# Tokens on 64 lanes of 7: q on even and k on odd partitions, chunks of 128 keys, one chunk shared by two heads

## The chip, the cores and the metric

One core of one Trainium2 chip. The metric is the device time of one execution in microseconds (us). The engines are called PE (TensorE), DVE (VectorE), ACT (ScalarE), POOL (GpSimd) and SP (SyncE).

## The reference

```python
# q, k, v: (8 batches, 12 heads, 448 tokens, 64); g_q, g_k: (64,)
def rmsnorm(x, g):
    return x / np.sqrt(np.mean(x * x, axis=-1, keepdims=True) + 1e-06) * g
scores = rmsnorm(q, g_q) @ rmsnorm(k, g_k).transpose(0, 1, 3, 2) / 8
attn   = softmax(scores)                       # over the keys
x      = (attn @ v) -> (3584 tokens, 768)
h = x @ w_in                                   # (768, 2048)
out = (h * sigmoid(1.702 * h)) @ w_out         # (2048, 768), float32
```

## The kernel before

The work is cut into 48 units, each two heads of one batch. A unit's q, k and v are loaded as float32, q and k are normed to bf16 and turned (by PE in the first 12 units, by a transposing DMA in the later 36), scores are taken key by query, ACT takes the exponential, PE multiplies with v and a column of ones, DVE divides, and the result is turned back as the input of the two products of the MLP. A list scheduler written into the kernel fixes the order of all instructions on every engine from estimated durations and searched tables of keys. The framework then adds the waits that the data need.

The 448 tokens of a head lie on 112 partitions, four in each. Landing buffers of the first units lie in one large tile, `late`, with turned q and k and with values ready for PE. Later the same tile holds terms of the second product.

```python
late = consts.tile([128, 3 * T_LEN + N_SUM * S_LEN], BF16, name="late", tag="late")
def piece(n, dtype=BF16): ...                   # the next n columns of late
early_raw  = [piece(4 * NS * D, FP32)... for _ in range(2)]   # q/k land here
early_vraw = [piece(2 * NS * D, FP32)... for _ in range(3)]   # v lands here
qkw_ring  += [piece(KW) for _ in range(N_KZ - K_KZ)]          # turned q and k
vx_ring   += [piece(2 * NS * (D + 1))... for _ in range(N_V - K_V)]
# ... cut ...
def load(i, which):
    src = (q, k, v)[which][b, h0:h0 + 2].rearrange("h (ss ns) d -> ss h ns d", ns=NS)
    if which == 2:
        nc.sync.dma_start(out=vraw[...][:SS], in_=src)          # SS = 112
        return
    eng = nc.scalar if i == 0 and which == 1 else nc.sync
    eng.dma_start(out=raw[...][:SS, which], in_=src)
# ... cut ...
def take_q(i):                                  # units turned by PE
    nc.vector.tensor_copy(out=qk_ring[...][:, 0], in_=tps[i][:, 0])
def take_k(i):
    nc.vector.tensor_scalar(out=qk_ring[...][:, 1], in0=tps[i][:, 1],
                            scalar1=gG[:, :], scalar2=None, op0=ALU.mult)
# ... cut ...
def score(u, t):                                # two heads on half the rows each
    for hp in range(2):
        r = slice(64 * hp, 64 * hp + 64)
        nc.tensor.matmul(sc[:, hp, ...], lhsT=qkw[r, k0:k0 + WIN], rhs=qk[r, 0, qs], ...)
```

Of the kernel before, what the change touches and what calls it, by code (L numbers as in the profile page):

```python
# [9 lines left out]
FP32 = mybir.dt.float32  # L10
# [16 lines left out]
class _Order:  # L27
# [36 lines left out]
    def run(self):  # L64
# [32 lines left out]
        def share():  # L97
            n = len(heads())
            return 1.3 / 2 if n == 2 and not queues["sw"] else 1.0 / n

        def next_moved():
            h = heads()
            when = [q[0].there for q in queues.values() if q and q[0].there > moved_to]
            when += [moved_to + t.rest / share() for t in h]
            return min(when) if when else None

        def move_to(now):
            nonlocal moved_to, seq
            while moved_to < now:
# [3 lines left out]
                for t in h:  # L113
                    t.rest -= (until - moved_to) * share()
# [109 lines left out]
    'g': 14.22, 'gT': -28.28, 'gG': 10.29, ('S', 0, 0): 33.65, ('R', 0, 0): -27.2, ('S', 0, 1):  # L224
    11.09, ('R', 0, 1): 12.24, ('Q', 0): 30.36, ('N', 0, 0): -6.12, ('N', 0, 1): -30.37, ('V',
    0): -7.89, ('T', 0, 0): -31.78, ('T', 0, 1): -29.53, ('KQ', 0): -10.97, ('K', 0): -11.43,
    ('S', 1, 0): 9.57, ('R', 1, 0): -27.21, ('S', 1, 1): 33.28, ('R', 1, 1): 9.51, ('Q', 1):
    33.27, ('N', 1, 0): 9.56, ('N', 1, 1): 11.7, ('V', 1): -5.89, ('T', 1, 0): 57.36, ('T', 1,
    1): 54.48, ('KQ', 1): -6.09, ('K', 1): -5.86, ('S', 2, 0): 32.41, ('R', 2, 0): -5.94, ('Q',
    2): 15.94, ('N', 2, 0): -4.94, ('N', 2, 1): -13.33, ('V', 2): 10.47, ('T', 2, 0): 55.3,  # L230
    ('T', 2, 1): 17.1, ('KQ', 2): -6.5, ('K', 2): -4.7, ('S', 3, 0): -3.51, ('R', 3, 0): -11.44,
    ('Q', 3): 33.8, ('N', 3, 0): -27.91, ('N', 3, 1): -14.89, ('V', 3): -5.47, ('T', 3, 0):
    19.15, ('T', 3, 1): 18.23, ('KQ', 3): 58.1, ('K', 3): -9.14, ('S', 4, 0): 33.8, ('R', 4, 0):
    57.84, ('Q', 4): 34.16, ('N', 4, 0): 23.2, ('N', 4, 1): 9.27, ('V', 4): -10.25, ('T', 4, 0):
    -3.92, ('T', 4, 1): 18.9, ('KQ', 4): -7.69, ('K', 4): 59.82, ('S', 5, 0): 18.65, ('R', 5,
    0): -7.68, ('Q', 5): 22.81, ('N', 5, 0): 1.27, ('N', 5, 1): 43.71, ('V', 5): -16.35, ('T',
    5, 0): -40, ('T', 5, 1): 16.66, ('KQ', 5): -8.39, ('K', 5): -9.71, ('L', 6, 0): 54.32, ('L',
    6, 1): 54.14, ('L', 6, 2): 54.15, ('S', 6, 0): -24.61, ('R', 6, 0): -9.13, ('N', 6, 0):
    -16.87, ('N', 6, 1): -1.42, ('V', 6): -24.19, ('T', 6, 0): -37.32, ('T', 6, 1): 56.1, ('KQ',
    6): -17.12, ('K', 6): -15.91, ('L', 7, 0): 55.06, ('L', 7, 1): 57.25, ('L', 7, 2): 55.05,  # L240
    ('S', 7, 0): -17.15, ('R', 7, 0): 31.45, ('N', 7, 0): 3.06, ('N', 7, 1): -23.94, ('V', 7):
    -24.2, ('T', 7, 0): 52.6, ('T', 7, 1): 22.24, ('KQ', 7): -20.86, ('K', 7): 9.99, ('L', 8,
    0): 54.79, ('L', 8, 1): 57.74, ('L', 8, 2): 53.4, ('S', 8, 0): 44.16, ('R', 8, 0): 31.27,
    ('Q0', 8): -1.5, ('Q', 8): -10, ('N', 8, 0): 3.5, ('N', 8, 1): 19.46, ('V', 8): -20.98,
    ('T', 8, 0): 27.35, ('T', 8, 1): 59.99, ('KQ', 8): -20.38, ('K', 8): -21.01, ('L', 9, 0):
    53.95, ('L', 9, 1): 55.46, ('L', 9, 2): 55.45, ('S', 9, 0): -9.31, ('R', 9, 0): -17.4, ('N',
    9, 0): -3.91, ('N', 9, 1): -10.14, ('V', 9): 22.05, ('T', 9, 0): -32.5, ('T', 9, 1): -35.1,
    ('KQ', 9): 21.57, ('K', 9): -38.08, ('L', 10, 0): 57.72, ('L', 10, 1): 59.75, ('L', 10, 2):
    60, ('S', 10, 0): -10.41, ('R', 10, 0): 19.25, ('N', 10, 0): 27.28, ('N', 10, 1): -1.35,
    ('V', 10): -15.43, ('T', 10, 0): -30.6, ('T', 10, 1): -36.19, ('KQ', 10): -4.09, ('K', 10):  # L250
    -37.28, ('L', 11, 0): 59.99, ('L', 11, 1): 59.99, ('L', 11, 2): 55.44, ('S', 11, 0): -13.26,
    ('R', 11, 0): 29.44, ('Q0', 11): 25.43, ('Q', 11): -9.79, ('N', 11, 0): 24.78, ('N', 11, 1):
    3.73, ('V', 11): 3.33, ('T', 11, 0): -37.35, ('T', 11, 1): -37.08, ('KQ', 11): -32.1, ('K',
    11): 24.13, ('C', 0, 0, 0): -31.61, ('E', 0, 0, 0): 59.86, ('C', 0, 0, 1): -26.54, ('E', 0,
    0, 1): 56.76, ('P', 0, 0, 0, 0): 53.97, ('P', 0, 0, 0, 1): -27.58, ('P', 0, 0, 0, 2):
    -30.53, ('P', 0, 0, 0, 3): -27.58, ('O', 0, 0, 0): -5.47, ('B', 0, 0): -40, ('X', 0, 0):
    -11.15, ('C', 1, 0, 0): -26.72, ('E', 1, 0, 0): -2.87, ('C', 1, 0, 1): 57.55, ('E', 1, 0,
    1): 16.48, ('P', 1, 0, 0, 0): 18.9, ('P', 1, 0, 0, 1): 18.63, ('P', 1, 0, 0, 2): 18.63,
    ('P', 1, 0, 0, 3): 18.89, ('O', 1, 0, 0): -13.5, ('B', 1, 0): 20.2, ('X', 1, 0): -11.33,
    ('C', 2, 0, 0): -40, ('E', 2, 0, 0): 18.66, ('C', 2, 0, 1): 20.21, ('E', 2, 0, 1): 13.02,  # L260
    ('P', 2, 0, 0, 0): 15.34, ('P', 2, 0, 0, 1): -36.54, ('P', 2, 0, 0, 2): -39.14, ('P', 2, 0,
    0, 3): -39.14, ('O', 2, 0, 0): -0.47, ('B', 2, 0): -39.81, ('X', 2, 0): -5.02, ('C', 3, 0,
    0): 17.29, ('E', 3, 0, 0): 39.33, ('C', 3, 0, 1): -39.63, ('E', 3, 0, 1): 38.35, ('P', 3, 0,
    0, 0): 15.85, ('P', 3, 0, 0, 1): 43.01, ('P', 3, 0, 0, 2): 17.41, ('P', 3, 0, 0, 3): 18.15,
    ('O', 3, 0, 0): -10.7, ('B', 3, 0): 15.63, ('X', 3, 0): 0.44, ('C', 4, 0, 0): -4.69, ('E',
    4, 0, 0): 38.96, ('C', 4, 0, 1): 38.48, ('E', 4, 0, 1): 24.48, ('P', 4, 0, 0, 0): -33.37,
    ('P', 4, 0, 0, 1): 60, ('P', 4, 0, 0, 2): -31.73, ('P', 4, 0, 0, 3): 17.26, ('O', 4, 0, 0):
    0.31, ('B', 4, 0): 57.93, ('X', 4, 0): 41.32, ('C', 5, 0, 0): -31.71, ('E', 5, 0, 0): 17.88,
    ('C', 5, 0, 1): 15.57, ('E', 5, 0, 1): 35.94, ('P', 5, 0, 0, 0): 33.77, ('P', 5, 0, 0, 1):
    33.77, ('P', 5, 0, 0, 2): 33.77, ('P', 5, 0, 0, 3): 33.76, ('O', 5, 0, 0): -0.04, ('B', 5,  # L270
    0): -23.85, ('X', 5, 0): 33.63, ('C', 0, 1, 0): 14.17, ('E', 0, 1, 0): 39.32, ('C', 0, 1,
    1): -39.73, ('E', 0, 1, 1): 33.79, ('P', 0, 1, 0, 0): -36.96, ('P', 0, 1, 0, 1): -33.38,
    ('P', 0, 1, 0, 2): 60, ('P', 0, 1, 0, 3): -14.87, ('O', 0, 1, 0): 60, ('B', 0, 1): 54.78,
    ('X', 0, 1): 34.24, ('C', 1, 1, 0): -36.97, ('E', 1, 1, 0): -39.74, ('C', 1, 1, 1): -36.95,
    ('E', 1, 1, 1): 24.11, ('P', 1, 1, 0, 0): 33.76, ('P', 1, 1, 0, 1): -23.7, ('P', 1, 1, 0,
    2): -22.7, ('P', 1, 1, 0, 3): -23.86, ('O', 1, 1, 0): -21.46, ('B', 1, 1): -39.64, ('X', 1,
    1): 0.33, ('C', 2, 1, 0): -27.46, ('E', 2, 1, 0): -31.49, ('C', 2, 1, 1): -18.62, ('E', 2,
    1, 1): 37.85, ('P', 2, 1, 0, 0): -39.65, ('P', 2, 1, 0, 1): -40, ('P', 2, 1, 0, 2): 21.69,
    ('P', 2, 1, 0, 3): -40, ('O', 2, 1, 0): -14.64, ('B', 2, 1): -36.82, ('X', 2, 1): -4.18,
    ('C', 3, 1, 0): 55.19, ('E', 3, 1, 0): 37.86, ('C', 3, 1, 1): 60, ('E', 3, 1, 1): 23.18,  # L280
    ('P', 3, 1, 0, 0): -18.63, ('P', 3, 1, 0, 1): -13.68, ('P', 3, 1, 0, 2): -13.69, ('P', 3, 1,
    0, 3): -11.57, ('O', 3, 1, 0): 39.32, ('B', 3, 1): 22.25, ('X', 3, 1): -18.47, ('C', 4, 1,
    0): -15.41, ('E', 4, 1, 0): 9.01, ('C', 4, 1, 1): -25.6, ('E', 4, 1, 1): -9.3, ('P', 4, 1,
    0, 0): -36.38, ('P', 4, 1, 0, 1): -36.83, ('P', 4, 1, 0, 2): -36.39, ('P', 4, 1, 0, 3):
    -34.65, ('O', 4, 1, 0): -20.37, ('B', 4, 1): 20.64, ('X', 4, 1): 22.61, ('C', 5, 1, 0):
    -16.67, ('E', 5, 1, 0): 42.7, ('C', 5, 1, 1): 51.97, ('E', 5, 1, 1): 36.5, ('P', 5, 1, 0,
    0): 47.97, ('P', 5, 1, 0, 1): 48.4, ('P', 5, 1, 0, 2): 60, ('P', 5, 1, 0, 3): 55.7, ('O', 5,
    1, 0): 25.18, ('B', 5, 1): -40, ('X', 5, 1): 21.57, ('C', 6, None, 0): 24.44, ('E', 6, None,
    0): -11.29, ('E', 6, None, 1): -16.82, ('C', 6, None, 2): 24.41, ('E', 6, None, 2): -7.71,
    ('E', 6, None, 3): -16.82, ('P', 6, None, 0, 0): -40, ('P', 6, None, 0, 1): -40, ('P', 6,  # L290
    None, 0, 2): -40, ('P', 6, None, 0, 3): -39.93, ('O', 6, None, 0): 23.74, ('P', 6, None, 1,
# [46 lines left out]
def kernel(  # L338
# [100 lines left out]
    for t in vx_ring:  # L439
        nc.gpsimd.memset(t[:, :, :, D:D + 1], 1.0)  # L440
# [784 lines left out]
```

## Time and profile before

| | before |
|---|---|
| median of 4 runs beside the changed kernel | 428.89 us (428.02 to 429.21) |
| span of the profiled execution | 426.3 us |
| mean granted clock of PE | 0.998 |
| first exponential of ACT | 11.12 us |
| first projection on PE (L875) | 35.13 us |
| last matmul ends | 422.0 us |

The prediction below shows the page, the stretches and the chain of PE from which it argues. Three kinds of numbers recur. *Busy* time of PE counts fillers (matmuls on zeros that the kernel places in planned gaps) and overlapping ends too. *Start-to-start distances* in the timeline give what a matmul really costs. *PE idle by accounting*, which is my own sum, is the start-to-start time of each pair of matmuls less the cost of the first (columns at 2.4 a ns plus 2.5 ns, half of that for each of a pair on half the rows, 0.09 us for a change between half and full array).

### The profile page before, as it was taken

How to read it: one execution, taken by the hardware profiler on the slowest of the kernel's cores; microseconds unless marked ns; L12 is line 12 of the kernel's file. 1: busy time of each engine (PE TensorE's matmuls, PEld its weight loads, DVE VectorE, ACT ScalarE, POOL GpSimd, SP SyncE). 2: the span in 40 equal slices, each digit the busy share in tenths (PEclk: the TensorE clock that was granted, in tenths of full speed). 3: DMA queues.
4: the chain of work that ended last, by engine and by line, in shares of the span. 5: the costliest groups of instructions: out<-in, count | busy, mean ns of one | idle time of the engine just before them, and what ended most of it. 6: DMA issues, size and time to landing. Idle time of an engine off the chain costs nothing.

```text
span 426.3 us, 10048 instructions
## 1 busy us (share of the span) xinstructions
PE 409.1 (96%) x3874; PEld 241.7 (57%) x3874; DVE 297.3 (70%) x584; ACT 302.6 (71%) x437; POOL 189.8 (45%) x277
## 2 busy tenths in 40 slices
PE   6899899999989999999999999999999999999995
PEld 4558686655555555555555555555555555565553
DVE  5967988579988677965787577764676555655663
ACT  4898788869978699978986589867775477604400
POOL 6396853657387473854636355553642100000000
PEclk9999999999999999999999999999999999999999
DMA  8999999575559989667636687556333630121023
GB/s 224 248 257 245 258 246 248 141 161 129 134 124 205 219 196 208 155 166 156 170 103 160 156 227 165 136 136 169 74 77 95 157 90 13 23 67 38 0 75 92
DMA packets 101555, 63.38 MB, mean 149 GB/s; under 512 B 54916, under 2 KB 101508, under 8 KB 101508
## 3 DMA queue, kind: packets, MB, share of 16 engines
q1 hardware_dynamic: 93712, 55.88, 53.9%
q0 software_dynamic: 7296, 6.29, 9.0%
q8 instruction: 30, 0.49, 0.5%
q10 hardware_dynamic: 500, 0.57, 0.4%
q14 instruction: 17, 0.14, 0.1%
HBM read 45.61 MB, written 11.01 MB: 133 GB/s over the span
## 4 chain that ended last, share of the span: by engine, by line
PE 78%; DVE 11%; ACT 5%; issue 3%; DMA 2%; POOL 0%; DVEq 0%
PE w L875 30%; PE w L965 17%; PE o L664 10%; PE sc L643 9%; PE sc L965 4%; PE w L905 4%; DVE late L956 4%; PE sc L875 2%; ACT att L653 2%; ACT sq L525 1%; DVE ssq L534 1%; DVE obs L675 1%; DVE g L897 1%; DMA raw<-in_k_dram 1%; DVE w_out_s L945 1%
## 5 line engine op out<-in xcount | busy, mean ns | idle before, releaser
L651 ACT ACTIVATE att<-sc 112x896 bf16<-112x896 f32 x168 | 145.8, 917 | 33.4 <-PE sc L643 32.9
L875 PE MATMUL w<-xt,w_in_s 128*128 128x448 bf16 (+1 forms) x810 | 150.7, 330 | 0.1
L875 PEld LDWEIGHTS <-w_in_s 128*128 128x128 bf16 x864 | 78.1, 97 | 54.2 <-issue 6.7
L576 POOL TENSOR_TENSOR row<-raw,rs 112x512 bf16<-112x512 f32 x80 | 89.5, 1139 | 25.8 <-DMA qk<-row 13.5
L664 PEld LDWEIGHTS <-att 112*128 112x128 bf16 x1536 | 72.5, 98 | 49.3 <-issue 18.2
L897 DVE SCALAR_TENSOR_TENSOR g<-th,w 128x448 bf16<-128x448 f32 x119 | 72.5, 616 | 26.8 <-ACT th L885 26.3
L885 ACT ACTIVATE th<-w 128x448 f32<-128x448 f32 x119 | 64.6, 548 | 26.3 <-PE w L875 24.7
L664 PE MATMUL o<-vx,att 112*128 112x65 bf16 x1280 | 74.2, 194 | 4.9 <-DVE obs L675 4.7
L589 POOL TENSOR_TENSOR vx<-vraw,ones 112x512 bf16<-112x512 f32 x35 | 36.5, 1042 | 95.0 <-PE o L664 59.4
L534 DVE TENSOR_REDUCE ssq<-sq 112x16 f32<-112x1024 f32 (+1 forms) x50 | 58.5, 1171 | 10.4 <-ACT sq L525 9.8
L525 ACT ACTIVATE sq<-raw 112x1024 f32<-112x1024 f32 (+1 forms) x43 | 44.5, 1036 | 11.2 <-DMA raw<-in_k_dram 7.0
L643 PE MATMUL sc<-qk 64*128 64x448 bf16 (+1 forms) x360 | 46.9, 342 | 1.6 <-DVE qk L606 1.4
L675 DVE TENSOR_TENSOR obs<-o,rcp 112x256 bf16<-112x256 f32 x96 | 40.8, 425 | 3.3
L965 PEld LDWEIGHTS <-g 128*128 128x128 bf16 x336 | 29.9, 97 | 19.6 <-issue 3.0
L674 DVE RECIPROCAL rcp<-o 112x4 f32<-112x4 f32 x96 | 17.1, 178 | 33.0 <-PE o L664 32.4
L965 PEld LDWEIGHTS <-late 128*128 128x128 bf16 x328 | 28.8, 97 | 18.3 <-issue 2.6
L965 PE MATMUL w<-w_out_s,g 128*128 128x384 bf16 x176 | 33.5, 325 | 0.0
L965 PE MATMUL w<-w_out_s,late 128*128 128x384 bf16 x152 | 29.7, 326 | 0.2 <-DVE late L956 0.2
L965 PE MATMUL w<-late 128*128 128x384 bf16 x144 | 28.1, 326 | 0.0
L978 DVE TENSOR_SCALAR osb<-w 128x384 f32<-128x384 f32 x25 | 13.9, 557 | 16.8 <-PE w L965 16.8
L617 ACT ACTIVATE qk<-qk,gG 128x448 bf16<-128x448 bf16 x36 | 24.2, 676 | 0.3 <-DMA qk<-row 0.3
L566 POOL TENSOR_TENSOR t<-rs 112x48 f32<-112x48 f32 x28 | 8.2, 292 | 35.8 <-DVE rs L555 34.7
(92 smaller groups left out, 379.7 us busy)
## 6 DMA issues: line engine op xcount, KB each, us to landing
raw<-in_q_dram SPq DMA_DIRECT2D x44, 224.0 KB, 3.7
raw<-in_k_dram SPq DMA_DIRECT2D x43, 224.0 KB, 4.7
vraw<-in_v_dram SPq DMA_DIRECT2D x42, 224.0 KB, 3.7
w_in_s<-in_moe_w_in_dram POOLq DMA_DIRECT2D x4, 768.0 KB, 15.8
w_out_s<-in_moe_w_out_dram POOLq DMA_DIRECT2D x4, 768.0 KB, 21.2
out_dram<-osb SPq DMA_DIRECT2D x14, 168.0 KB, 2.4
out_dram<-osb SPq DMA_DIRECT2D x12, 144.0 KB, 2.6
out_dram<-osb SPq DMA_DIRECT2D x12, 120.0 KB, 2.5
```

Of the source, the lines that this page charges most:

```text
L525: nc.scalar.activation(out=sq[i % N_SQ][:SS, part], in_=raw[turn(i, N_RAW, K_RAW)][:SS, part], func=ACT.Square)
L534: nc.vector.reduce_sum(out=ssq_of[g0][:SS, i - g0, part], in_=sq[i % N_SQ][:SS, part], axis=AX.X)
L576: eng.tensor_tensor(out=row_ring[i % N_QKN][:SS, gi].rearrange("p n (h d) -> p h n d", h=2), in0=raw[turn(i, N_RAW, K_RAW)][:SS, gi], in1= ...
L589: nc.gpsimd.tensor_tensor(out=vx[:, :, :D], in0=vr, in1=ones[:SS, :].to_broadcast([SS, 2 * NS, D]), op=ALU.mult)
L643: nc.tensor.matmul(sc[:, hp, j * SH:j * SH + n], lhsT=qkw[r, k0:k0 + WIN], rhs=qk[r, 0, qs], start=True, stop=True)
L651: nc.scalar.activation(out=att[:SS, t, :, :S], in_=sc, func=ACT.Exp)
L664: nc.tensor.matmul(os_[u, w][:, x, :], lhsT=att_of(u)[:SS, kc, hp, qs * SS:qs * SS + WIN], rhs=vx_ring[turn(i, N_V, K_V)][:SS, hp, kc, :], ...
L675: nc.vector.tensor_tensor(out=to[:SS, :, w, :] if h is None else to[:SS, :2].rearrange("p n h d -> p (n h) d"), in0=o[:SS, :, :D], in1=rcp ...
L875: nc.tensor.matmul(gps[b, m][:, j * SH:j * SH + n], lhsT=w_in_s[:, ki, f * 128:(f + 1) * 128], rhs=xT[b][:, ki, lo:lo + n], start=(ki == 0 ...
L885: nc.scalar.activation(out=th[:, :], in_=gps[b, m][:, :S], func=ACT.Tanh, scale=0.851)
L897: nc.vector.scalar_tensor_tensor(out=g_of[b // 2][:, f:f + len(g), lo:lo + n], in0=view(ths.pop((b, m))[:, :]), scalar=1.0, in1=view(gps.p ...
L965: nc.tensor.matmul(held[to], lhsT=lhs[:, ko, :], rhs=y[:, ko, :], start=first and ko == 0, stop=ko == NK - 1, skip_group_check=not first)
```

## The change

Seven tokens lie on each of 64 lanes. q takes the even partitions and k the odd ones, so squares, norms and turns use all 128 partitions. Keys come in three chunks of 128 per head and one chunk of 64 keys of each head, which one full-array matmul scores for both heads. v is spread over 128 partitions in 8 slots, one of which is loaded twice and masked, so that 28 instead of 32 matmuls do a unit's values. Less work for ACT and PE was the aim, mainly in the first 35 us.

```diff
-    late = consts.tile([128, 3 * T_LEN + N_SUM * S_LEN], BF16, name="late", tag="late")
+    late = consts.tile([128, 3 * T_LEN + N_SUM * S_LEN + 1056], BF16, name="late", tag="late")
@@ loads @@
-            nc.sync.dma_start(out=vraw[turn(i, N_RAW, K_VRAW)][:SS], in_=src)
+            for side in range(2):
+                nc.sync.dma_start(
+                    out=vraw[turn(i, N_RAW, K_VRAW)][side::2].rearrange("p (h n) d -> p h (n d)", h=2),
+                    in_=bass.AP(tensor=src.tensor, offset=src.offset + side * four, ...))
-        eng.dma_start(out=raw[turn(i, N_RAW, K_RAW)][:SS, which], in_=src)
+        eng.dma_start(out=raw[turn(i, N_RAW, K_RAW)][which::2].rearrange("p h n d -> p h (n d)"), in_=src)
@@ turned q and k @@
+        qs = t[:, :S] if i < ON_PE else t[:, 0:2 * S:2]
-        nc.vector.tensor_copy(out=qk_ring[...][:, 0], in_=tps[i][:, 0])
+        nc.vector.tensor_copy(out=parts_of(i)[0], in_=tps[i].rearrange("p n s -> p (n s)")[:, 0::2])
+        both_heads(i, nc.vector, x)             # the shared keys, masked by head
@@ scores @@
+        for lo in whole:
+            nc.tensor.matmul(sc[:, 0, lo:lo + n], lhsT=apart, rhs=qs, start=True, stop=True)
@@ order @@
-            od.add(("L", i, w), ..., 460, ..., moves=900.0)
+            od.add(("L", i, w), ..., 1310 if w == 2 else 655, ..., moves=975.0 if w == 2 else 690.0)
-                   deps=[("T", i, 0)] + kz_free)              # the copy of q
+                   deps=[("T", i, 0), ("T", i, 1)] + kz_free)
```

Cut: exponentials, values, masks, norms and stores in the new layout, and the tables of keys, which were searched anew.

## The prediction

> **What bounds the kernel now.** I first read the page: busy shares, then slices. A profiled execution spans 426.3 us (the timed median is 429.0).
>
> ```profile
> PE 409.1 (96%) x3874; PEld 241.7 (57%) x3874; DVE 297.3 (70%) x584; ACT 302.6 (71%) x437; POOL 189.8 (45%) x277
> ...
> PE   6899899999989999999999999999999999999995
> ```
>
> TensorE is busy 96%, but that contains 89 filler matmuls on zeros (line 500) that only keep its clock up. So I next asked for the stretches: columns are the stretch, its length, busy time of PE, PEld, DVE, ACT, POOL, granted clock, DMA share, GB/s.
>
> ```profile
> 0.00:35.20 35.20, 29.11 (x365) 19.34 (x366) 25.96 (x59) 27.40 (x41) 21.96 (x42) 1.00 1.08 243
> 35.20:50.00 14.80, 13.00 (x188) 11.41 (x188) 12.02 (x29) 10.48 (x15) 10.40 (x16) 1.00 1.19 248
> 50.00:120.00 70.00, 69.89 (x735) 44.91 (x734) 56.63 (x110) 61.04 (x89) 39.68 (x60) 1.00 0.80 178
> 120.00:400.00 280.00, 275.12 (x2458) 153.15 (x2457) 187.95 (x364) 201.56 (x291) 117.77 (x161) 1.00 0.55 132
> ```
>
> From 50 us on PE hardly pauses; ACT (201.6 of 280) and POOL have room. Before 35.2 us, when the first projection (line 875) starts, it is different. Next the PE timeline (start, length, count), which gives the true cost of a matmul as the distance from start to start:
>
> ```profile
> 150.22 1.30 PE L875 MATMUL w<-xt,w_in_s 128*128 128x448 bf16 x6
> 151.36 0.42 PE L664 MATMUL o<-vx,att 112*128 112x65 bf16 x8
> 151.71 0.55 PE L643 MATMUL sc<-qk 64*128 64x448 bf16 x4
> 152.20 0.43 PE L664 MATMUL o<-vx,att 112*128 112x65 bf16 x8
> 152.47 2.43 PE L875 MATMUL w<-xt,w_in_s 128*128 128x448 bf16 x12
> ```
>
> Six 448-column matmuls take 1.14 us, 0.190 each. Eight values matmuls (65 columns) take 0.27 us where another full-array one follows (152.20 to 152.47), 0.034 each, and 0.35 where scores follow. Four score matmuls, two pairs on half the rows each, take 0.49, not 2 x 0.19 = 0.38. So a change between full and half array costs about 0.09 us each way. Fillers stand 0.110 apart, turns of 112 columns 0.049.
>
> With these costs the order of instructions gives 15.3 us of useful PE work before 35.2 us (48 turns 2.4, 128 values 4.4, 84 scores 4.5 plus 3.3 of switches, 14 turns back 0.7). **About 20 us of the first 35 are filler or idle.** After that I find 3 us idle up to 120 us and 6 us from 120 on, most of it here (waits of PE):
>
> ```profile
> PE o L664 <- DVE obs L675: 4.7, 7, 1.2
> ```
>
> The last matmul ends near 422, the span at 426.3: a tail of 4.3. Useful PE work is 426.3 - 20 - 3 - 6 - 4.3 = **393 us**.
>
> What holds the first 35 us? ACT's groups from 11 us (first exponential, 11.12) to 36.5 (first tanh, 36.49):
>
> ```profile
> L653 ACT ACTIVATE att<-sc 112x896 bf16<-112x896 f32 x21 | 17.9, 914 | 2.0 <-PE sc L643 1.9
> L525 ACT ACTIVATE sq<-raw 112x1024 f32<-112x1024 f32 x3 | 3.2, 1051 | 0.0
> L385 ACT ACT_TABLE_LOAD x1 | 1.3, 1283 | 0.0
> L545 ACT ACTIVATE ssq<-ssq,eps 112x16 f32<-112x16 f32 x4 | 1.2, 306 | 0.0
> ```
>
> Idle is 2 us, half of it before 11.12: ACT is the bound there. DMA is saturated too (about 250 GB/s to 75 us), but PE never waits on it, and ACT and POOL only before 5 us and once (3.6 us): it is prefetching.
>
> **What the Trainium skill says.** (1) "TensorEngine Tiling (Array Packing)", Key Properties: changing the tiling mode drains TensorE. The trace agrees: the 0.09 us above. (2) "TensorE: Matmul & The Clock Gate", Back-to-back issue gap: warm gap is N/2.4 + 2.5 ns. It agrees at 448 (189 against 190), and at 65 the trace decides (34). For 130 columns it gives 57 ns; the trace's 110 ns at 256 columns is in line. (3) "SBUF — State Buffer", the note on cachelines: 16-byte lines, at least two hits in each needed. The new q operand is read at every second bf16, four hits a line, so it should stay at full rate; no run shows this yet. (4) "VectorE: DVE Perf Modes", Mode 2x_1P: packed 16-bit reads need step 1. The q copy now takes 387 ns for 448 elements, which fits two a cycle; at step 2 it should lose that.
>
> **The change part by part.**
> PE, scores: per unit of two heads 3 pairs plus one full-array matmul of 448 columns instead of 4 pairs: four slots as before. The full one falls at the end of a group of pairs, so the number of switches stays. **0.**
> PE, values: 32 of 65 columns (32 x 0.034 = 1.09 us) become 24 of 65 and 4 of 130 (0.82 + 0.23 = 1.05). 0.036 x 48 units = **-1.7 us**, on the path. Turns: 8 x 0.049 against 7 x 0.056: 0.
> ACT: the exponential of 896 takes 0.917, tanh of 448 0.548, so 0.82 ns an element: the half unit's second (672) is 0.73, the full unit's fourth (448) 0.55. That is 36 x 0.37 = 13 us off, plus 0.1 us a square, but after 50 us ACT is not the bound: hidden. What counts is ACT before the first tanh. Old order: 21 exponentials at 0.86 (pairs overlap: 1.72 for two), 4 squares at 0.97, 4 Ln/Exp pairs at 0.5, table 1.28 = 25.2, against 25.4 seen. New order: 9 of 0.86, 10 of 0.68, 2 squares of 0.87, 3 pairs, table = 19.1. But one more square and Ln/Exp pair (1.4) now precede the first exponential: first tanh and projection 4.7 us earlier. Since fewer units are done by then, useful PE work ahead of it falls to about 14.0 (98 values, 66 scores): 1.3 us is only moved. Left 3.4; I count **-3**. Fillers fall from 89 to 77.
> DVE: sums of squares 1024 to 896, about -0.12 us x 50; early norms and casts move to POOL. Against it the shared keys (0.28 estimated from 150 cycles plus 128 at 0.96 GHz) and the q copy (+0.24), 12 times each. Spread over an engine at 67 to 75%: hidden, perhaps -0.3 on the 4.7 us of waits.
> POOL: 36 new small multiplications at 0.4 (estimate), 3 more squares; norms of 384 elements instead of 512 in half of the cases (-0.25 each). Near even.
> DMA: q and k come in 1792-byte pieces instead of 1024, v in two transfers with one slot of eight double. Hidden. The stores become two of 64 rows; tail as before.
> Sum: 426.3 - 1.7 - 3 - 0.3 = 421.3; with the 2.7 us between span and timed median **424.0 us**, ratio 0.988.
>
> **The rivals.** (a) POOL becomes the early bound: up to the first projections it now holds 10 of 12 norms and 4 casts against 6 and 2. For: its sums come to some 15 us between 7 and 23. Against: nothing else waits for it. It would eat the 3 us: 427. (b) Reading q at step 2 halves the moving rate: 4 x 0.19 x 36 = 27 us worse, 450. Against: four hits a line; I give it 2 to 3%. (c) The waits of values for the divided output are rearranged by the new fixed order, since there is still a single output bank: 6 us may become 3 or 9: 421 to 427. (d) The early phase shrinks by more, because ACT, DVE and DMA are all relieved at once: of 20 us, some 10 are unavoidable (first useful matmul at 9.3), so at most 8 more: 416 to 419.
>
> **Range and chances.** (c) alone is plus or minus 3, (a) and (d) move it by +3 to -6: 8 in 10 between 419.0 and 428.5. Faster by over 2% means under 420.4, which needs (d) or a good (c): 0.15. Slower means over 437.6: only (b): 0.03. Within 2%: 0.82.
>
> **What would show it.** Values: 1152 matmuls of 65 at 34 ns and 192 of 130 at 57 ns. Scores still 0.49 per four from the second slot on; if 0.8, (b). First tanh near 32 us with ACT without gaps; if ACT waits there with POOL rows as releasers, (a). Last-element exponential 0.55 us; ACT's total down by about 17 us with no effect after 50 us. PE waits on line 754's output near 4.7 us. Wrong would be: useful PE work not near 391, or the early idle not near 17.

## More of the kernel before

Lines such as L741 are lines of the kernel that was profiled.

The queue of SP was not looked at closely in the prediction. This is what it does in the middle of before (timeline of SP: start, length, what; `x2` is two in a row):

```profile
195.40 0.53 SPq L515 DMA_DIRECT2D vraw<-in_v_dram  x1
195.98 0.45 SPq L518 DMA_DIRECT2D raw<-in_q_dram  x1
196.48 0.45 SPq L518 DMA_DIRECT2D raw<-in_k_dram  x1
```

The length is the time that SP spends on *issuing* the transfer, not the time of the transfer. All issues together take SP 165.5 us of the 306 us after 120 us.

## The result

| | before | after |
|---|---|---|
| median of 4 runs | 428.89 us (428.02 to 429.21) | 478.12 us (476.58 to 479.13) |
| ratio, 95% interval | | 1.1148 (1.1114 to 1.1183) |
| span of the profile | 426.3 us | 476.3 us |
| granted clock | 0.998 | 0.938 |
| first exponential, first projection | 11.12, 35.13 us | 17.20, 69.72 us |

The result is correct, and 49 us slower. Every ratio here is the mean time of one kernel's fast runs over that of before's fast runs in the same rounds, so it is not quite the ratio of the medians quoted.

The page of after, busy shares and the slices of PE and of its clock (each slice is 11.9 us):

```profile
PE 421.2 (88%) x3604; PEld 250.1 (53%) x3604; DVE 295.3 (62%) x600; ACT 280.3 (59%) x431; POOL 203.5 (43%) x322
...
PE   4833388399999999998899999999999999999996
...
PEclk9756579789999999999899999999999999999999
```

Most of the loss is in the first six slices, and there the clock falls too, to half in some stretches. The same stretches as the prediction showed (length, busy PE, PEld, DVE, ACT, POOL, clock, DMA share, GB/s):

```profile
0.00:35.20 35.20, 17.97 (x142) 11.82 (x143) 16.60 (x38) 14.82 (x26) 17.59 (x39) 0.75 0.70 192
35.20:50.00 14.80, 6.91 (x54) 4.34 (x53) 4.24 (x12) 2.43 (x4) 7.01 (x6) 0.62 0.56 118
50.00:120.00 70.00, 51.39 (x580) 39.30 (x579) 42.44 (x94) 36.53 (x53) 29.75 (x41) 0.82 0.76 162
120.00:400.00 280.00, 273.69 (x2349) 154.45 (x2347) 190.12 (x382) 201.52 (x306) 147.03 (x236) 0.99 0.64 149
```

No engine is busy for much more than half of either stretch before 50 us (PE 17.97 of the first 35.20 us), and the transfers slowed too: 192 and 118 GB/s where before moved 243 and 248. So neither a busier engine nor a fuller DMA explains it; something waits. The waits of PE in after (total, times, longest) say for what:

```profile
PE o L741 <- DMA late<-in_v_dram: 13.3, 3, 8.1
PE w L637 <- POOL row L619: 9.0, 2, 8.1
PE sc L707 <- DMA late<-in_v_dram: 7.9, 1, 7.9
```

This is strange. L707 are scores: they read turned q and k, which DVE writes; L741 are values, which read v as DVE or POOL has cast it. Neither reads what a DMA has loaded. But all of these lie in the tile `late`, where the landing buffers lie too, in other columns. The queue of SP, from the start to 75 us, shows the same in the other direction:

```profile
SPq L554 <- PE sc L707: 9.0, 1, 9.0
...
SPq L554 <- POOL att L474: 3.6, 1, 3.6
```

A load waits 9 us for scores, and the very first load waits 3.6 us for memsets, which write other columns. The built program confirms it without a chip: the weights of a score in `late` carry waits on six DMA semaphores (a semaphore is the counter by which a transfer or an engine tells others that it is done).

```
L707 Ldweights late [waits DMAHW3,DMAHW5,DMAHW2,DMAHW6,DMAHW1,DMAHW0]
```

The trace of after carries the same: just before the score at 37.78 us PE's queue waits on six different DMA semaphores. In before, the only PE instructions of the first 75 us that wait on a DMA semaphore read loaded weights (L875, L905). And when the slices `[which::2]` and `[side::2]` are replaced by contiguous ones, these waits vanish from the program; in the trace of that run (halves, below) they are absent too.

### The profile page after: what moved, and what is told of

The parts are those of the page before. It is cut to its first block, busy times and chain, and to the rows that moved or that the text cites. A ratio compares the mean times of both kernels' runs of the same rounds, so it can differ in the third digit from the quotient of the medians.

```text
span 476.3 us, 9605 instructions
## 1 busy us (share of the span) xinstructions
PE 421.2 (88%) x3604; PEld 250.1 (53%) x3604; DVE 295.3 (62%) x600; ACT 280.3 (59%) x431; POOL 203.5 (43%) x322
## 4 chain that ended last, share of the span: by engine, by line
PE 71%; DMA 10%; DVE 6%; issue 4%; SPq 3%; POOL 2%; ACT 2%; POOLq 0%; DVEq 0%; ACTq 0%
PE w L960 24%; PE w L1044 18%; PE o L744 6%; PE sc L707 6%; DMA late<-in_v_dram 4%; PE sc L1044 4%; PE w L990 3%; DMA raw<-in_k_dram 3%; PE o L741 3%; PE sc L710 3%; PE sc L960 2%; DVE late L1035 2%; SPq L548 2%; POOL row L619 1%; DVE ssq L571 1%
## 5 line engine op out<-in xcount | busy, mean ns | idle before, releaser
L719 ACT ACTIVATE att<-sc 128x896 bf16<-128x896 f32 (+1 forms) x168 | 130.2, 825 | 54.6 <-PE sc L707 54.2
L619 POOL TENSOR_TENSOR row<-raw,rs 128x384 bf16<-128x384 f32 (+1 forms) x85 | 84.2, 1011 | 0.9 <-issue 0.5
L626 POOL TENSOR_TENSOR vx<-vraw,v_of_head 128x512 bf16<-128x512 f32 x36 | 38.8, 1079 | 84.1 <-PE o L744 49.3
L744 PEld LDWEIGHTS <-att 128*128 128x128 bf16 x1152 | 63.7, 101 | 18.9 <-issue 2.8
L571 DVE TENSOR_REDUCE ssq<-sq 128x14 f32<-128x896 f32 (+1 forms) x50 | 51.9, 1043 | 27.0 <-ACT sq L562 26.2
L744 PE MATMUL o<-vx,att 128*128 128x65 bf16 x960 | 65.6, 196 | 0.0
L562 ACT ACTIVATE sq<-raw 128x896 f32<-128x896 f32 (+1 forms) x40 | 37.2, 933 | 23.8 <-DMA raw<-in_k_dram 13.4
L707 PE MATMUL sc<-qk 64*128 64x448 bf16 (+1 forms) x270 | 41.7, 363 | 0.2 <-ACT att L719 0.2
L741 PEld LDWEIGHTS <-att 128*128 128x128 bf16 x192 | 19.2, 100 | 41.8 <-issue 12.3
L741 PE MATMUL o<-vx,att 128*128 128x130 bf16 x160 | 36.2, 226 | 4.0 <-DVE obs L754 3.3
L1057 DVE TENSOR_SCALAR osb<-w 128x384 f32<-128x384 f32 x29 | 16.2, 557 | 21.8 <-PE w L1044 21.7
```

What stands on the lines that cost most here:

```text
L571: nc.vector.reduce_sum(out=ssq_of[g0][:, i - g0, part], in_=sq[i % N_SQ][:, part], axis=AX.X)
L619: eng.tensor_tensor(out=row_ring[i % N_QKN][:, gi:NT:2].rearrange("p n (h d) -> p h n d", h=2), in0=raw[turn(i, N_RAW, K_RAW)][:, :, ns], ...
L626: eng.tensor_tensor(out=vx_ring[turn(i, N_V, K_V)][:, :, :D], in0=vraw[turn(i, N_RAW, K_VRAW)][:, :, :], in1=v_of_head[:, :].to_broadcast( ...
L707: nc.tensor.matmul(sc[:, hp, lo:lo + n], lhsT=ks[r, c * WIN:(c + 1) * WIN], rhs=qs[r], start=True, stop=True)
L719: nc.scalar.activation(out=o, in_=sc[:, :, :S] if t < NC else sc[:, 0, :S], func=ACT.Exp)
L741: nc.tensor.matmul(o[:, x:x + 2, :], lhsT=att_of(u)[:, NT - 2, qs * SS:qs * SS + WIN], rhs=vx[:, NC:NC + 2, :], start=True, stop=True)
```

## The experiments

18 kernels were run, each beside before on the same chip. All gave a correct result but the two that are marked wrong.

### First question: is it the shared tile?

**tiles_apart.** The changed kernel, landing buffers in three tiles of their own; partition steps, tables and everything else stay. Terms of the second product that had lain there are placed in these tiles later.

```diff
-    late = consts.tile([128, 3 * T_LEN + N_SUM * S_LEN + 1056], ...)
+    late = consts.tile([128, 2 * T_LEN + S_LEN], ...)
+    early_r = [consts.tile([128, 4 * NT * D], BF16, ...) for j in range(2)]
+    early_v = consts.tile([128, T_LEN], BF16, ...)
```

> The changed kernel with one thing undone: the early landing buffers of q, k and v become tiles of their own instead of pieces of the shared tile late (each term of the later product moves with them). Loads, layout, partitions, order of all instructions stay. Theory A (a load that steps over every second partition of late is taken by the build to touch all of late, so loads and all users of late wait for one another without need): PE's waits on DMA late<-in_v (13.3 and 7.9 us) and the SP queue's waits of 8 to 10 us vanish, the clock stays near 1.0, time 415 to 430 us. Rival B (the loads themselves are too slow, four DMAs a unit instead of three, eight in flight): the waits stay and only change name, 465 to 480. Rival C (the new fixed order issues loads too late): also 465 to 480.

Measured: 436.3 us (435.24 to 439.7), ratio 1.0193 (1.0146 to 1.0239), span 433.4, clock 0.99. 42 of the 49 us are gone, and no PE instruction waits long on a DMA any more.

**halves.** The other way out: `late` stays shared, but q lies on partitions 0 to 63, k on 64 to 127, and v in contiguous halves, so there is no partition step.

```diff
-                    out=vraw[...][side::2]...
+                    out=vraw[...][LN * side:LN * side + LN]...
-        eng.dma_start(out=raw[...][which::2]...
+        eng.dma_start(out=raw[...][LN * which:LN * which + LN]...
     # reads of turned q and k in runs of 64 to match
```

> The changed kernel, correct, with q on partitions 0 to 63 and k on 64 to 127 (v likewise in two contiguous halves) instead of even and odd ones; late stays shared. Theory A: no step over partitions, so no false waits: 415 to 430 us, same as tiles_apart within 3 us. B and C: as slow as the changed kernel, 465 to 480. A side question: q now lies in runs of 64 contiguous bf16, so if the step of 2 costs TensorE the 300 ns from a pair to the full score matmul and the 210 ns after the full one should fall to about 282 and 189, some 2 us in all against tiles_apart; if a transfer into 64 neighbouring partitions is slower, landing times of raw rise above 3.5 us and early waits on DMA appear.

Measured: 440.33 us (439.71 to 441.53), ratio 1.028 (1.0257 to 1.0303). The long waits are gone here too, with the tile shared as in after. But both times lie above the 415 to 430 us expected, and 4 us apart instead of within 3: these waits are not all of the loss.

**before_step** and its control **before_split.** In the kernel *before*, only the loads into `late` are cut in two: every second partition (step) or the two contiguous halves (split). Bytes, number of transfers and order are the same in both.

```diff
+        for lanes in (slice(0, SS, 2), slice(1, SS, 2)) if shared else (slice(0, SS),):        # step
+        for lanes in (slice(0, SS // 2), slice(SS // 2, SS)) if shared else (slice(0, SS),):   # split
+            eng.dma_start(out=to[lanes] ..., in_=src[lanes])
```

> The kernel before, correct, with one thing added: loads into late are issued as two DMAs over every second partition (56 each). Nothing else of the change. Theory A: the same false waits arise (PE users of late wait on up to eight DMA semaphores), 440 to 480 us, clock below 0.98, PE waits on DMA late above 8 us. Rivals B and C, which need the new loads or the new order: at most 2 us above before, 428 to 431.

> Control of before_step: the same 14 loads also as two DMAs of 56 partitions, but each over contiguous ones. Theory A: no false waits, 427 to 432 us (the 20 extra DMAs cost at most 3 us of issue). If merely splitting loads costs (rival B), it is as slow as before_step.

Measured: before_step 478.23 us (478.13 to 478.76), ratio 1.116 (1.1143 to 1.1176); before_split 430.71 us (428.48 to 433.2), ratio 1.005 (1.0008 to 1.0093). The old layout with stepped loads is as slow as the whole change. The waits of PE in before_step:

```profile
PE sc L643 <- DVE qk L606: 14.6, 2, 14.2
PE sc L643 <- DMA late<-in_k_dram: 9.7, 1, 9.7
PE o L664 <- DMA late<-in_v_dram: 7.6, 2, 3.9
PE sc L643 <- DMA late<-in_v_dram: 7.5, 1, 7.5
```

So the first cause is shown from both sides: a partition-stepped transfer into a part of a tile makes readers and writers of *other columns* of that tile wait. It is not the amount of work in the new layout. That the build's tracking of such slices is coarse is read from the waits in the built program; that they cost some 42 us is measured.

### Second question: where do 8 us more come from in tiles_apart?

By accounting PE idles 13.4 us after 120 us in tiles_apart, 7.3 in before. The chain there runs: a gate of DVE waits in its queue behind a sum of squares, that for a square of ACT, and that for k (waits of ACT for squares, 120 to 400 us; this is before):

```profile
ACT sq L525 <- DMA raw<-in_k_dram: 5.5, 6, 1.5
```

The same view of tiles_apart:

```profile
ACT sq L565 <- DMA raw<-in_k_dram: 15.2, 10, 2.8
```

What ACT waits for is a load that SP issued late. The timeline of SP in tiles_apart:

```profile
202.14 0.67 SPq L557 DMA_DIRECT2D raw<-in_q_dram  x1
202.85 0.66 SPq L557 DMA_DIRECT2D raw<-in_k_dram  x1
...
207.30 1.26 SPq L551 DMA_DIRECT2D vraw<-in_v_dram  x2
```

An issue over 64 partitions takes 0.60 us or more (median 0.605), where one over 112 took 0.45 (q, k) or 0.53 (v), although it has fewer and larger pieces. v now needs two. Loads of a unit cost SP 2.4 instead of 1.4 us. After 120 us SP spends 206.8 us on issues instead of 165.5. Loads make 31 us of the difference; stores, now of 64 rows each, make 14 (an issue of theirs went from 0.42 to 0.59 us, median), and transposes take 4 less. The Trainium skill names this kind of limit ("Perfetto Trace Analysis", What "DMA-bound" means: the issuing sequencer as a bound of its own, to which it says large descriptors are what matter). The page speaks of a sequencer that does nothing but issue; here SP issues for only 198 of the 280 us between 120 and 400 us, but loads stand in its order behind other issues and come late. With the second part the trace disagrees: for the same 224 KB of q or k, fewer and larger pieces came with the longer issue.

**v_on_act** and **v_on_pool.** tiles_apart; from the 13th unit on v's two loads are issued from another queue. Only the issuing engine changes; order is the same.

```diff
-                nc.sync.dma_start(
+                (nc.sync if i < ON_PE else nc.scalar).dma_start(      # v_on_pool: nc.gpsimd
```

> tiles_apart (early landing buffers in tiles of their own) with one more edit: from the 13th unit on the two loads of v are issued from ScalarE's queue instead of SyncE's; the order of all other work is unchanged. tiles_apart ran 436.3 us (ratio 1.0193). Theory S: what is left of the slowdown (about 8 us against before) comes from SyncE's queue: an issue of 64 partitions takes 0.60 us there (before: 0.45 for q or k, 0.52 for v), so a unit costs it 6.3 us with transposes and stores instead of 4.8, and q and k land late. Then, with 36 x 1.21 = 44 us of issues gone from SyncE, ScalarE's squares wait for q and k much less after 120 us (15.2 us in tiles_apart, 5.5 in before), TensorE's waits for the gate go from 3.8 us to under 2, and the time falls to 430 to 433.5. Rival W: the rest is work and order of the new layout (scores at step 2, the retuned order); then the time stays at 436 plus or minus 1. Rival X: ScalarE's own time for 44 us of issues delays exponentials and tanh, and it gets slower, 438 or more.

> As v_on_act, but the two loads of v are issued by GpSimd from the 13th unit on. Theory S: SyncE is relieved in the same way, 430 to 433.5, if GpSimd (busy 43% there) can spare the time of the issues (its two loads of weights took about 1 us each, so some 2 us a unit). Rival W: 436 plus or minus 1. Rival X: GpSimd's norms and casts come late, PE waits on rows or values: 438 or more.

Measured: v_on_act 436.37 us (432.79 to 439.11), ratio 1.0169 (1.012 to 1.0219); v_on_pool 450.63 us, ratio 1.0511 (1.0488 to 1.0534). By the time alone theory S (SP's queue makes the rest) had failed. By stretch it had not: in v_on_act idle after 120 us fell from 13.4 to 7.3 us and squares waited 2.3 us for k, but 6.9 us of idle came up between 50 and 70 us. The timeline of ACT in v_on_act shows why:

```profile
54.30 3.10 ACTq L551 DMA_DIRECT2D vraw<-in_v_dram  x2
57.50 1.73 ACT L722 ACTIVATE att<-sc 128x896 bf16<-128x896 f32 x2 [3.48 <-DVE obs L757]
```

Two loads hold ACT's queue for 3.1 us, and the exponentials behind them wait. On POOL it was worse: PE waited up to 9.6 us for POOL's norms. A load moved to another queue takes that engine's time and its place in order.

**v_act_late.** So the move is made only from the 21st unit on (`nc.scalar if i >= 20`), after that crowded stretch.

> v_on_act with the v loads moved to ScalarE's queue only from the 21st unit on. In v_on_act the waits after 120 us fell as theory S says (TensorE idle there 13.4 to 7.3 us by start-to-start accounting, squares' wait for k 15.2 to 2.3), but 6.9 us of idle came up between 50 and 70 us, where one moved load blocked ScalarE for 3.1 us and others delayed exponentials and tanh. Theory S: without those, idle after 120 us near 7.5 and nothing lost at 50 to 70: 429.5 to 431.5, ratio about 1.004. Rival W (rest is work and order): 436 plus or minus 1.

Measured: 430.34 us (428.89 to 434.8), ratio 1.0072 (1.0026 to 1.0118). Idle after 120 us is 6.8 us, squares wait 0.8 us for k, and SP issues for 170.0 us. The 6 us come from v's loads in SP's queue.

**before_issue.** The same from the other side: before, every load cut in two over 56 neighbouring partitions.

```diff
-        eng.dma_start(out=raw[...][:SS, which], in_=src)
+        for s in (slice(0, 56), slice(56, 112)): eng.dma_start(out=raw[...][s, which], in_=src[s])
```

> The kernel before, every load of q, k and v cut into two transfers of 56 neighbouring partitions each, nothing else; same bytes, no partition steps. SyncE's issues of a unit rise from about 1.4 us to 1.9 to 2.7 us (an issue takes 0.31 to 0.46). Theory S: loads come later, squares wait more for them, and the time rises by 3 to 8 us to 432 to 437, without waits of TensorE on transfers. Rival W: SyncE's queue has room in the old layout and only latency counts: 429 plus or minus 1.5 (with a quarter of these loads cut, the control before_split was 1.005).

Measured: 443.04 us (441.81 to 445.52), ratio 1.0344 (1.0315 to 1.0373). SP's issues after 120 us rise to 199.8 us, squares wait 12.8 us for k, idle there is 13.1 us; the first projection comes at 42.90 us. The direction is as expected and the size twice that, mostly before 50 us. Smaller transfers may have a part in it; the run does not separate them from the issues.

**before_v_act.** The mend of v_act_late in the kernel before.

> The kernel before with v loads from the 21st unit on issued by ScalarE's queue, nothing else. It tells whether SyncE's queue cost time in the old layout too. Theory S says only where loads come late: squares wait 5.5 us for k after 120 us there, and TensorE's idle of 7.3 us is mostly for divided outputs, so 0 to -1.5 us: 427 to 429. If it fell by 4 us or more, the gain of v_act_late would say nothing on the new layout's issues.

Measured: 429.47 us (428.79 to 431.64), ratio 1.002 (0.9995 to 1.0045). The old layout had room in SP's queue; moving loads gains nothing there. So v_act_late did mend something that the change had brought. (The move also puts v into a second queue, while before_issue also makes transfers smaller: no run lengthens the issue alone.)

**start_mended** and **v_act_first.** tiles_apart with q of the 7th unit issued after the loads of four units (`load(6, 0)` held back until `load(4, 0)`); and tiles_apart with v of the first four units issued by ACT (`nc.scalar if i < 4`).

> tiles_apart with one load moved: the q of the 7th unit, which the retuned order issues first on SyncE's queue, is issued after the loads of the first four units. Theory S: its 0.8 us of issue and its transfer stand ahead of the first q; first square at about 4.5 us instead of 5.35, first turn of TensorE 0.8 to 1 us earlier, time 435.3 to 435.8. Rival: the start is set by the gain vectors or k of the first unit instead, and nothing moves: 436.3 plus or minus 0.7.

> tiles_apart with the v loads of the first four units on ScalarE's queue, which idles before 10 us; order otherwise unchanged. In the first 50 us SyncE spends 34.0 us on issues (before: 24.1). Theory S: q and k of units 2 to 8 are issued 1.2 to 4.8 us sooner, first projection 1 to 3 us before 35.5 us, time 433.5 to 435.5. Rival: the early phase is set by something else (ScalarE, or the order), or the fixed order eats the gain: first projection at 35.5, 436.3 plus or minus 1.

Measured: start_mended 435.83 us (435.52 to 438.19), ratio 1.0186 (1.0162 to 1.021): not to be told from tiles_apart, though the first square came at 4.77 instead of 5.35 us. v_act_first 434.23 us (433.44 to 436.14), ratio 1.014 (1.0112 to 1.0168): the time is inside what was expected, but the first projection stayed at 35.52 us, so not by the way expected.

**all_mended.** tiles_apart, the load moved, v of units 1 to 4 and from 21 on issued by ACT.

> tiles_apart with all three mends: v of units 1 to 4 and from 21 on issued on ScalarE's queue, and q of the 7th unit after the first four units' loads. Theory S: 428 to 431, level with before (428.9). If the change also gives what was predicted for the early phase once loads come in time, 425 to 427.

Measured: 429.17 us (428.35 to 431.76), ratio 1.0025 (0.9993 to 1.0057). Level with before. The two causes account for the whole slowdown; the gain that was predicted is still missing.

### Third question: what does the step of 2 in q cost?

**q_step1.** tiles_apart; scores of the later 36 units read neighbouring columns of q. Its output is wrong, which doesn't matter for the time.

```diff
-        qs = t[:, :S] if i < ON_PE else t[:, 0:2 * S:2]
+        qs = t[:, :S]
```

> tiles_apart, but the scores of the later 36 units read q as 448 neighbouring columns instead of every second one. The result is WRONG on purpose (other columns are read); nothing else moves. If reading at step 2 costs what the trace of the changed kernel suggests (a pair 207 ns against 197, the full-array score after a pair 300 against 292, the next one 210 against 200: about 0.05 us a unit), the time falls by 1.5 to 2.5 us to about 434.3, and the distances return to 197, 292 and 200. If those distances come from something else (a stall in the pairs' banks), nothing changes: 436.3 plus or minus 0.7. Rival (b) of the prediction, half rate, would show as 20 us less.

Measured: 437.32 us (433.96 to 438.7), ratio 1.0188 (1.0146 to 1.0229): the time cannot tell. The start-to-start distances of the trace can (ns, median after 120 us):

| from, to | tiles_apart (step 2) | q_step1 (step 1) |
|---|---|---|
| pair of scores, full-array score | 300 | 292 |
| pair of scores, values | 287 | 281 |
| full-array score, projection | 210 | 200 |

A read at step 2 costs 6 to 10 ns for 448 columns, and the halved rate of the prediction's rival (b) is out. The trace of halves, which reads neighbouring columns and is correct, agrees: 292, 281 and 200. The 282 and 189 that were expected there did not come, so the rest of 292 and 200 is not the step.

### Fourth question: why does the early phase not shrink?

**q_on_act.** In the chain of v_act_first DVE's copies of q and k stand where ACT's exponentials stood in before. They became longer (DVE's groups in the first 50 us of before: count, busy us, mean ns of one, idle ahead of them):

```profile
L606 DVE TENSOR_SCALAR qk<-w,gG 128x448 bf16<-128x448 bf16 x6 | 2.7, 444 | 0.1
L603 DVE COPY qk<-w 128x448 bf16<-128x448 bf16 x6 | 2.2, 387 | 0.7 <-PE w L599 0.5
```

The same groups of tiles_apart:

```profile
L656 DVE TENSOR_SCALAR qk<-w,gG 128x384 bf16<-128x384 bf16 x4 | 2.6, 644 | 0.0
L652 DVE COPY qk<-w 128x448 bf16<-128x448 bf16 x4 | 2.5, 622 | 1.1 <-PE w L640 1.0
```

So all_mended was run with the 12 copies of q on ACT (`nc.scalar.activation(..., func=ACT.Identity)` in `take_q`).

> all_mended (early buffers apart, v loads of units 1 to 4 and from 21 on issued by ScalarE, the misplaced load moved) with one more edit: the 12 early copies of q out of the turned block are done by ScalarE instead of VectorE; order otherwise unchanged. Theory V: with the loads mended, the first 35 us follow VectorE: in the chain of waits of v_act_first the copies of q (0.62 us; before 0.39), k (0.64; before 0.45) and the shared keys (0.28; none before) of the early units stand one after another between 13 and 29 us, where in before ScalarE's exponentials stood. Then taking 0.62 us x 8 units before the first projection off VectorE brings it 2 to 4 us before the 36.05 us of all_mended, and the time falls from 429.2 to 425.5 to 427.5. Rival: ScalarE, in order, delays exponentials for these copies, or PE's fixed order sets the phase: first projection within 1 us of 36, 428.5 to 430.5.

Measured: 434.84 us (432.99 to 435.77), ratio 1.013 (1.0105 to 1.0155). Slower than all_mended. DVE now waited 7.8 us for these copies, and a load of v at the head of ACT's queue held ACT for 3.3 us at 10.6 us, so the run says little of DVE.

**short_copies** and **q_on_act_late.** Two cleaner tries on v_act_late: copies of q and multiplications of k on neighbouring columns (wrong, same engine), and the copies of q on ACT without early loads there.

```diff
-        ... in_=tps[i].rearrange("p n s -> p (n s)")[:, 0::2])
+        ... in_=tps[i].rearrange("p n s -> p (n s)")[:, :S])
-        ... out=parts_of(i)[1].rearrange("p (c s e) -> p c e s", ...), in0=lanes(x[...])[:, 1], ...
+        ... out=parts_of(i)[1], in0=x[:, :NC * WIN], ...
```

> v_act_late with the 12 early copies of q and the 12 multiplications of k reading and writing neighbouring columns instead of every second one: WRONG result on purpose, same amounts, same engine, same order. They should take 0.39 and 0.41 us instead of 0.62 and 0.64 (as in halves). Theory V (the early phase follows VectorE's copies once loads are mended): 0.46 us times the 8 or so units before the first projection, so it comes 1.5 to 3.5 us before the 35.14 us of v_act_late and the time falls from 430.3 to 427 to 429. Rival: the phase is set by loads, by the start or by PE's fixed order; the copies' time turns into idle of VectorE: first projection within 0.7 us of 35.1, 429.5 to 431.5.

> v_act_late with the 12 early copies of q on ScalarE. In q_on_act a load of v at the head of ScalarE's queue held it for 3.3 us at 10.6 us and the copies behind it, so that run says little of VectorE; here no early load is on ScalarE. Theory V: first projection 1 to 3 us before 35.14, 427.5 to 429.5. Rival (ScalarE in fixed order makes k's multiplication wait for the copy before it, as VectorE waited 7.8 us for these copies in q_on_act): first projection later than 36, 431 or more.

Measured: short_copies 430.79 us (428.69 to 431.68), ratio 1.0025 (0.9996 to 1.0054), first projection 34.64 us; q_on_act_late 430.99 us (430.3 to 432.61), ratio 1.0042 (1.0018 to 1.0067), first projection 36.63 us. Shorter copies (389 and 408 ns) brought 0.5 us at the first projection, against 1.5 to 3.5 expected. Theory V (DVE as the early bound) is not borne out. It is no clean zero: the times' intervals overlap that of v_act_late, and the trace of short_copies has a stretch at half clock of 6.8 us from 10.5 us on, that of v_act_late one of 3.4.

**halves_mended.** No partition step anywhere, tiles apart, v from unit 21 on issued by ACT: meant to beat both.

> A correct version meant to beat both: q on partitions 0 to 63, k on 64 to 127, v in contiguous halves (no partition step anywhere), early buffers in their own tiles, v loads from unit 21 on issued by ScalarE. Copies 0.39 and 0.41 us, scores at step 1 (2 us less by the distances), ScalarE's scaling of k 0.62 instead of 0.73. Against it, loads into 64 neighbouring partitions landed later in halves (q 4.3, k 5.1 us after issue, against 3.7 and 4.0 in tiles_apart). If theory V and the distances hold: 425 to 427.5. If the slower landing eats it: 429 to 433.

Measured: 433.69 us (430.77 to 435.0), ratio 1.0096 (1.0062 to 1.013). It does not. The first square comes at 6.42 us (v_act_late 5.42) and the first projection at 37.01. In halves, q and k landed 4.3 and 5.1 us after their issue (median), in tiles_apart 3.7 and 4.0. So in these traces even and odd partitions were the better choice for landing; why, the runs do not show.

**few_fillers.** v_act_late without the 35 filler matmuls planned after 14 us.

```diff
-        n = idle * FILL / 213 if now < 14000.0 else idle * FILL_GAPS / 110
+        n = idle * FILL / 213 if now < 14000.0 else 0
```

> v_act_late without the 35 filler matmuls (0.110 us each, 3.9 us) that the list places in PE's planned gaps from 14 us on; those before 14 us stay, order otherwise unchanged. In short_copies theory V fell: VectorE's copies were shorter, yet the first projection only came 0.5 us earlier and the time stayed. What the traces now say is that the phase from the first exponential to the first projection did shrink as predicted (24.0 us in before, 21.1 in v_act_late), but the first exponential comes 3 us later (14.07 against 11.12). Theory F: what is left is held by PE itself, fillers standing in its fixed order where data would already be there; then the first projection comes 1.5 to 3.5 us before 35.14 and the time is 427 to 429. Rival: the fillers only stand where PE would idle anyway; then idle takes their place, 430 to 431.5; if PE's clock drops for lack of them, later still.

Measured: 430.47 us (429.42 to 431.86), ratio 1.0034 (1.0006 to 1.0061). The first projection comes at 36.62 us, later, and idle between 12 and 40 us rises from 7.2 to 12.3 us by accounting. But the clock fell as well (stretch 19.7 to 29.9 us, columns as above; v_act_late, then few_fillers):

```profile
19.70:29.90 10.20, 8.58 (x123) 5.99 (x122) 8.76 (x22) 8.38 (x12) 7.58 (x7) 1.00 1.08 267
19.70:29.90 10.20, 8.94 (x86) 6.01 (x86) 8.66 (x20) 7.39 (x12) 7.24 (x8) 0.50 1.01 257
```

Without the fillers PE ran at half clock there, so much of that "idle" is slower matmuls. The run shows that taking the fillers out does not help; whether they stand in the way at full clock (theory F) it leaves open.

What all of these traces agree on is this (us; each row is one profiled execution, so tenths mean little):

| | first square | first exponential | first projection | from exponential to projection |
|---|---|---|---|---|
| before | 4.17 | 11.12 | 35.13 | 24.0 |
| tiles_apart | 5.35 | 15.06 | 35.48 | 20.4 |
| start_mended | 4.77 | 13.47 | 35.47 | 22.0 |
| v_act_late | 5.42 | 14.07 | 35.14 | 21.1 |
| all_mended | 4.98 | 15.44 | 36.05 | 20.6 |
| short_copies | 5.39 | 14.54 | 34.64 | 20.1 |
| few_fillers | 5.46 | 14.47 | 36.62 | 22.1 |

The phase that ACT's exponentials fill did become 2 to 4 us shorter, and it starts 2.4 to 4.3 us later. Its work on ACT in v_act_late, from 14 to 35.2 us:

```profile
L727 ACT ACTIVATE att<-sc 128x896 bf16<-128x896 f32 x9 | 8.2, 915 | 1.6 <-PE sc L710 1.5
L731 ACT ACTIVATE att<-sc 128x672 bf16<-128x672 f32 x9 | 6.6, 729 | 1.4 <-PE sc L713 1.4
```

14.8 us, against the 17.9 us of 21 exponentials in before: the relief is there. But ACT now waits 3 us for scores within it, and the start eats the rest. One thing more sets these traces apart: each of the new layout's has a stretch at half clock before 30 us, 3.4 us or more (v_act_late from 9.3 us, all_mended 6.8 us from 11.6), and before has none. There turns stand 0.11 us apart instead of 0.05. What this costs was not tested.

## Why the prediction was wrong

**What bounds the kernel, before.** The reading of PE was right and carried through: with the waits mended, the stretch after 120 us is again PE's. The sentence on DMA failed: "PE never waits on it ... it is prefetching". True of before, it was taken over to after as if the change could not alter it.

**PE, scores: 0.** Mis-sized, little. Pair to pair went from 197 to 207 ns, pair to values from 282 to 287; the group that ends with the full-array score takes 300 + 210. Per unit: 2 x (197 + 282) = 958 ns became 207 + 287 + 300 + 210 = 1004, so +46 ns, 1.7 us over 36 units.

**PE, values: -1.7 us.** Right in mechanism, somewhat small (its own distances give 0.042 us a unit and 2.0 in all, where it wrote 0.036 and 1.7): 65 columns stand 32 to 33 ns apart, 130 columns 58, where it had taken 57 from the Trainium skill ("TensorE: Matmul & The Clock Gate", Back-to-back issue gap). 32 x 33 = 1.06 us became 24 x 32 + 4 x 58 = 1.00, 2.7 us over 48 units. Together with the scores about -1 us, where -1.7 was said.

**ACT, the early phase: -3 us.** The relief came (24.0 to 21.1 us from the first exponential to the first projection in v_act_late). The term that failed is the start: 1.4 us were allowed for one more square and Ln/Exp pair, and it is 3 us, 14.07 against 11.12. 1.25 us of it lie before the first square (4.17 to 5.42), where a load not yet needed is issued first and issues are longer; 1.7 us after it. Of these, 0.8 us lie between the first square and the first turn (11.36 in v_act_late, 9.30 in before). That turn starts 0.05 us after the end of a norm on POOL (1.04 us long, the second in a row there), in all six traces of the new layout in the table above; in before it followed a norm of 0.67 us on DVE. Another 0.8 us lie between the first turn and the first score (2.20 us against 1.41): the copy of q waits for all turns now, and the copies are longer. That split is read from traces; which part a better order could take back was not tried, and no experiment got the phase to end earlier than 34.6 us. Why is open.

**DVE: hidden.** Right as far as the runs go, since short_copies brought no change of time clear of noise, and by luck in part: the copy of q grew by 0.24 us as said (387 to 622 ns; it lost what "VectorE: DVE Perf Modes", Mode 2x_1P, grants at step 1 only) and the shared keys took 0.28, but the multiplication of k went from 444 to 644 ns for fewer columns, which the prediction did not see.

**POOL: near even.** Its busy time rose from 189.8 to 203.5 us in after. What was missed is where the work stands: the norm that the first turn waits for is now one of POOL's. No run moved it back. v_on_pool shows that POOL has no 2 us a unit to give.

**DMA: "q and k come in 1792-byte pieces instead of 1024, v in two transfers with one slot of eight double. Hidden."** This is the step that failed, twice, and it made the result. It counted bytes and pieces. It did not ask what else such a transfer touches: as partition-stepped writes into a tile shared with other data they brought waits worth some 42 us (tiles_apart, halves, before_step). And it did not ask what an issue costs SP: 0.60 instead of 0.45 us, and four instead of three a unit, worth 6 us after 120 us (v_act_late, before_issue).

**The rivals.** (b) half rate and (d) a larger gain did not come; (a) POOL as bound came in small, in the norm before the first turn (in all_mended PE waits 2.4 us for it); (c), the rearranged waits for the divided output, stayed small (3.3 us of `obs` waits in after against 4.7). All four were drawn from the old set of dependencies. A rival in which the new access pattern makes new dependencies was missing, though the diff of the program's waits could have shown it before any run: it needs no chip, only the comparison of which semaphores an instruction waits on.

The half clock in the early slices goes with the waits: PE waits up to 8 us at a stretch, and the granted clock is 0.5 for 44.3 of the first 75 us in after, for 37.5 in before_step, for 6.9 in tiles_apart and never in before. How much of the 42 us it makes was not measured alone.

No version beat before: all_mended (429.17 beside 428.63 us) is level with it.

## What to carry to other kernels

When a change alters the *shape* of an access to a tile that other data share, above all to every second partition, compare the waits of the built program before and after; give such landing buffers tiles of their own. Count a transfer's issue as work of the engine whose queue issues it, in the order of that queue, and look at that queue's timeline before calling a load hidden. And where an engine is relieved only in one phase, size the start of the phase as carefully as its length.

## What the Trainium skill lacked or had wrong

- No page has it that a partition-stepped slice of a tile makes instructions on other columns of that tile wait: 478.23 us with every second partition, 430.71 with halves, same bytes (before_step, before_split).
- "Perfetto Trace Analysis", What "DMA-bound" means, gives large descriptors as what matters for the issuing sequencer. Here, for the same 224 KB, an issue of 128 pieces of 1792 bytes over 64 partitions took SP 0.605 us and one of 224 pieces of 1024 bytes over 112 partitions 0.45 us. Half of v with 128 pieces of 1024 bytes took 0.61 us too. What sets the issue time the runs do not show.
- The same page, DMA Optimizations, proposes to balance DMAs over the queues of several engines. It gained 6 us from the 21st unit on, but nothing in all from the 13th on, and lost 14 us on POOL (430.34, 436.37, 450.63 us against 436.3): the issuing engine's place in order is missing there.
- "SBUF — State Buffer", the note on cachelines, would have a bf16 read at step 2 be free. It costs 6 to 10 ns per 448 columns as PE's moving operand.
